# Retention and maxout FFN on one core: transposes moved, weight sums gathered in the first tile, the last product by token blocks

## The chip, the cores and the metric

One core of a Trainium2 chip. The metric is the device time of one execution in microseconds (us). Executions of one kernel spread over 0.5 to 4.3 us and the kernel before drifted from 832.8 to 835.7 us (medians) between sessions (four of the twelve experiments ran on a second chip, and are marked so), so small differences are read from the record's ratios and from positions inside the profiles.

Engine names in the profile: PE is TensorE (products), PEld its weight loads, DVE VectorE, ACT ScalarE, POOL GpSimd, SPq the queue of SyncE that issues the transfers here. "L435" is line 435 of that kernel's source; inserted lines shift the numbers between kernels, so the text gives the tile names too (x, dx, down, osb).

## The reference, cut to what matters

```python
# q, k, v: (8, 8, 576, 64) float32; w1, w2, w3: (512, 768); w_out: (768, 512), float64
scores = scale * np.matmul(q, k.transpose(0, 1, 3, 2))
ret = scores * Dmat                       # causal, decaying with distance
attn = np.matmul(ret, v)                  # -> x: 4608 tokens x 512
h = np.maximum(np.maximum(x @ w1, x @ w2), x @ w3)
return h @ w_out                          # 4608 x 512
```

## The kernel before

Attention runs in 36 chunks of 128 tokens, the FFN in 9 tiles of 512 tokens. The float64 weights arrive as bit patterns and are converted to float32 by VectorE, ScalarE and GpSimd while the first tile is computed in the plain way; the other eight tiles use sums and differences of weight blocks (seven products instead of eight). In the traces each engine runs its instructions in the order in which the program lists them: in the kernel before, ScalarE's copies of the fourth chunk start at 23.30 us, behind the conversion's passes at 21.92 and 22.68. The parts that matter here (cuts marked):

```python
BY_PE = 8     # chunks 0..7: q and k transposed by TensorE; later chunks by VectorE

def load(g):
    rows = (("k", k), ("q", q), ("v", v)) if g < BY_PE else (("k", k), ("v", v))
    for n, src in () if g < BY_PE else (("q", q), ("kx", k)):
        # [cut] 16 transfers of 16 KB each, in the layout that VectorE's transpose needs
    for n, src in rows:
        # [cut] one or two transfers of whole rows; v comes last

def decay_values(g):          # GpSimd: vd = v * decay; needs v of the chunk

def downs(t, h):              # second half of the FFN for a tile: seven products
    def product(n, out, first):
        for fp in range(NF // 2):
            for m in range(NM):           # NM = 2 token blocks of 128
                nc.tensor.matmul(out[:, m, :], lhsT=..., rhs=..., start=first and m == 0 and fp == 0, ...)
    x = ps_x.tile([P, NM, DM // 2], FP32, tag="x", name="dx")   # both blocks: one PSUM tile
    # [cut]
    product(3, x, False)
    total(0, 1, x, [])        # ScalarE copies x to osb, one transfer of 256 KB to the output

# first tile, down products m = 0..3: weight sums of units [0], [1], [2], [3, 4];
# second tile: the sums of units 5..8, one per unit

warm(6); load(0); load(1)
nc.sync.dma_start(gs[:], state_decay); nc.sync.dma_start(gq[:], out_decay)
# [cut]
scores(2); convert(2); transposes(3); values(2); convert(2); scores(3)
```

## Time and profile before

| what | value | where it is read |
|---|---|---|
| median time | 832.78 us (3 runs), 833.6 us (6 runs) | timed runs |
| span of the profiled execution | 834.0 us | page, first line |
| TensorE busy | 823.8 us, 99% | page, part 1 |
| holes in TensorE | 2.0, 1.4, 1.4, 1.2, 0.7 us | list of waits |
| last product ends, span ends | 830.45, 834.0 us | chain of waits |

How to read it: TensorE is the bound, so another engine's time counts only where TensorE waits for it. The list of waits gives "who waited for whom: us in total, times, longest". In a timeline a line is "start, duration, engine, line, operation, out<-in, count", and square brackets hold the idle time of that engine just before and what ended it. The lines themselves are shown in the prediction.

### The profile page before, as it was taken

How to read it: one execution, taken by the hardware profiler on the slowest of the kernel's cores; microseconds unless marked ns; L12 is line 12 of the kernel's file. 1: busy time of each engine (PE TensorE's matmuls, PEld its weight loads, DVE VectorE, ACT ScalarE, POOL GpSimd, SP SyncE). 2: the span in 40 equal slices, each digit the busy share in tenths (PEclk: the TensorE clock that was granted, in tenths of full speed). 3: DMA queues.
4: the chain of work that ended last, by engine and by line, in shares of the span. 5: the costliest groups of instructions: out<-in, count | busy, mean ns of one | idle time of the engine just before them, and what ended most of it. 6: DMA issues, size and time to landing. Idle time of an engine off the chain costs nothing.

```text
span 834.0 us, 12632 instructions
## 1 busy us (share of the span) xinstructions
PE 823.8 (99%) x4626; PEld 670.5 (80%) x4626; DVE 427.3 (51%) x803; ACT 174.7 (21%) x395; POOL 186.7 (22%) x182
## 2 busy tenths in 40 slices
PE   8899999999999999999999999999999999999998
PEld 8545556788888888888888888888888888888887
DVE  3879946754355443554444445544545435533341
ACT  2656721111111101111111111111111011111211
POOL 3535545511211130212011111111111202201000
PEclk9999999999999999999999999999999999999999
DMA  8946521334133323332233313332333223201001
GB/s 220 283 131 188 133 58 40 57 56 84 50 55 56 56 59 65 67 56 55 60 55 73 67 48 56 57 57 80 56 57 54 59 60 73 48 13 38 1 1 50
DMA packets 232509, 59.06 MB, mean 71 GB/s; under 512 B 213504, under 2 KB 230912, under 8 KB 232448
## 3 DMA queue, kind: packets, MB, share of 16 engines
q1 hardware_dynamic: 232304, 58.26, 31.1%
q8 instruction: 36, 0.59, 0.3%
q14 instruction: 25, 0.20, 0.1%
q10 hardware_dynamic: 144, 0.00, 0.0%
HBM read 48.76 MB, written 9.44 MB: 70 GB/s over the span
## 4 chain that ended last, share of the span: by engine, by line
PE 95%; DMA 2%; DVE 1%; SPq 1%; ACT 0%; POOL 0%; issue 0%; DVEq 0%
PE x L435 30%; PE z L435 15%; PE dx L311 10%; PE y L435 7%; PE up L493 7%; PE dz L311 5%; PE s L183 4%; PE o L213 4%; PE o L218 4%; PE kv L194 4%; PE dy L311 2%; PE down L484 2%; SPq L152 1%; DMA bits<-in_moe_w_dram 1%; DMA gs<-in_state_decay_dram 1%; SPq L146 1%
## 5 line engine op out<-in xcount | busy, mean ns | idle before, releaser
L435 PE MATMUL x<-S,T 128*128 128x256 f32 x576 | 147.9, 379 | 0.0
L435 PEld LDWEIGHTS x<-S,T 128*128 128x128 f32 x576 | 109.1, 190 | 15.4 <-ACT p L440 0.3
L156 POOL TENSOR_TENSOR vd<-vraw,gk 128x512 f32<-128x512 f32 x36 | 37.8, 1049 | 344.9 <-DMA vraw<-in_v_dram 319.4
L435 PE MATMUL x<-S,w 128*128 128x256 f32 x288 | 74.5, 381 | 1.2 <-DVE h L465 1.2
L435 PE MATMUL x<-xT,w 128*128 128x256 f32 x288 | 74.8, 382 | 0.0
L435 PE MATMUL z<-S,w 128*128 128x256 f32 x288 | 73.9, 379 | 0.0
L435 PE MATMUL z<-xT,T 128*128 128x256 f32 x288 | 73.9, 379 | 0.0
L435 PE MATMUL y<-xT,w 128*128 128x256 f32 x288 | 73.9, 379 | 0.0
L465 DVE TENSOR_TENSOR tmp<-x,p 128x256 f32<-128x256 f32 x48 | 20.4, 425 | 103.4 <-PE x L435 103.4
L440 ACT COPY p<-x 128x256 f32<-128x256 f32 x72 | 26.8, 372 | 221.0 <-PE x L435 221.0
L186 DVE TENSOR_TENSOR st<-s,causal 128x512 f32<-128x512 f32 x72 | 46.3, 685 | 44.6 <-PE s L183 44.6
L493 PE MATMUL up<-xT,w 128*128 128x512 f32 x144 | 63.8, 595 | 1.4 <-POOL w L387 1.4
L435 PEld LDWEIGHTS x<-S,w 128*128 128x128 f32 x288 | 49.3, 189 | 14.8 <-DVE h L465 1.8
L435 PEld LDWEIGHTS z<-S,w 128*128 128x128 f32 x288 | 54.7, 190 | 7.4
L435 PEld LDWEIGHTS y<-xT,w 128*128 128x128 f32 x288 | 54.7, 190 | 7.4
L435 PEld LDWEIGHTS z<-xT,T 128*128 128x128 f32 x288 | 54.3, 189 | 7.9
L220 DVE TENSOR_TENSOR xT<-o,gq 128x512 f32<-128x512 f32 x36 | 24.8, 690 | 67.9 <-PE o L218 62.4
L435 PEld LDWEIGHTS x<-xT,w 128*128 128x128 f32 x288 | 51.5, 190 | 6.6 <-issue 0.8
L493 PEld LDWEIGHTS up<-xT,w 128*128 128x128 f32 x144 | 26.6, 190 | 32.2 <-issue 29.9
L294 POOL TENSOR_TENSOR H<-h 128x256 f32<-128x256 f32 x24 | 18.1, 756 | 150.7 <-DVE h L478 150.0
L440 ACT COPY u<-x 128x256 f32<-128x256 f32 x72 | 26.8, 372 | 99.8 <-PE x L435 97.1
L183 PEld LDWEIGHTS s<-qT,kT 64*128 64x128 f32 x576 | 35.0, 187 | 15.6 <-issue 11.7
(92 smaller groups left out, 1210.1 us busy)
## 6 DMA issues: line engine op xcount, KB each, us to landing
bits<-in_moe_w_dram SPq DMA_DIRECT2D x18, 512.0 KB, 4.7
out_dram<-osb SPq DMA_DIRECT2D x36, 256.0 KB, 2.1
kraw<-in_k_dram SPq DMA_DIRECT2D x32, 256.0 KB, 3.0
vraw<-in_v_dram SPq DMA_DIRECT2D x32, 256.0 KB, 3.5
qraw<-in_q_dram SPq DMA_DIRECT2D x448, 16.0 KB, 1.8
kxraw<-in_k_dram SPq DMA_DIRECT2D x448, 16.0 KB, 1.8
bits<-in_moe_w_out_dram SPq DMA_DIRECT2D x6, 512.0 KB, 3.4
qraw<-in_q_dram SPq DMA_DIRECT2D x7, 256.0 KB, 4.4
```

Source lines behind the costliest of these rows:

```text
L156: nc.gpsimd.tensor_tensor(t[:], raws.pop(("v", g))[:], gk[:].unsqueeze(2).to_broadcast([C, H, D]), op=ALU.mult)
L183: nc.tensor.matmul(s[j][:, p, :], lhsT=kT[r, p, :], rhs=qT[r, p, :], start=True, stop=True)
L186: nc.vector.tensor_tensor(st[:, j], s[j][:], masks[start_of(g)][:].unsqueeze(1).to_broadcast([C, NP, C]), op=ALU.mult)
L194: nc.tensor.matmul(kv[:, p, :], lhsT=pair(kr, p)[r:], rhs=pair(vds[g], p)[r:], start=True, stop=True)
L213: nc.tensor.matmul(o[D * j:D * (j + 1), p, :], lhsT=vr[:, 2 * p + j, :], rhs=st[:, j, p, :], start=(p == 0), stop=(old == 0 and p == NP - ...
L218: nc.tensor.matmul(o[:, p, :old], lhsT=sd[:, p, :], rhs=qT[:, p, :old], start=False, stop=(p == NP - 1), skip_group_check=True)
L220: nc.vector.tensor_tensor(xT[t][:, :, i * C:(i + 1) * C], o[:], gq[:], op=ALU.mult)
L311: nc.tensor.matmul(out[:, m, :], lhsT=hS[n](fp)[:, m * P:(m + 1) * P], rhs=late["T"][n][:, fp, :], start=first and m == 0 and fp == 0, sto ...
L435: nc.tensor.matmul(out[:], lhsT=w[:, d * P:(d + 1) * P], rhs=xS[t][n][:, d, :], start=first and d == 0, stop=d == 1, skip_group_check=True)
L440: nc.scalar.copy(c[:], src[:])
L465: nc.vector.tensor_tensor(c22, x[:], p7[:], op=ALU.add)
L493: nc.tensor.matmul(ps[:], lhsT=w_sb[i, fb][:, dc * P:(dc + 1) * P], rhs=xT[t][:, dc, :], start=(dc == 0), stop=(dc == NDC - 1))
```

## The change

Its intent: close the holes at the front, take one more chunk's transposes off TensorE, get the weight sums out of the second tile's way, and let the first half of the last output leave while the second half is computed. The diff, cut to its core:

```diff
-BY_PE = 8
+BY_PE = 7
-    def load(g):
+    def load(g, *between):
         for n, src in rows:
+            if n == "v":
+                for t, what in between:
+                    nc.sync.dma_start(t[:], what)
# downs(), last product
-        product(3, x, False)
-        total(0, 1, x, [])
+        osb = opool.tile([P, NM, DM // 2], FP32, tag="osb", name="osb")
+        for m in range(NM):
+            product(3, x, False, [m])
+            nc.scalar.copy(osb[:, m, :], x[:, m, :])
+            nc.sync.dma_start(place(0, 1)[:, m, :], osb[:, m, :])
# ffn()
-                if t == 1:
-                    weight_sums(n + 5)
-                for n in [[0], [1], [2], [3, 4]][m]:
+                for n in [[0, 1, 2], [3, 4, 5], [6], [7, 8]][m]:
# start
-    load(1)
-    nc.sync.dma_start(gs[:], state_decay)
-    nc.sync.dma_start(gq[:], out_decay)
+    load(1, (gs, state_decay), (gq, out_decay))
-    warm(3)
+    warm(2)
-    convert(2)
     transposes(3)
+    convert(2)
# [cut: the helper place(), the argument blocks of product()]
```

More of the change, by code (lines that the diff above doesn't have):

```diff
@@ L302, in summed, with product @@
             return lambda fp: late["S"][n][:, fp, :]
+        NM = NH // P
         hS = {1: raw_hidden(0, 0), 2: raw_hidden(0, 1), 3: summed(4), 4: raw_hidden(1, 1),
               5: summed(1), 6: summed(2), 7: summed(3)}
-        NM = NH // P
-        def product(n, out, first):
+        def product(n, out, first, blocks=range(NM)):
             for fp in range(NF // 2):
-                for m in range(NM):
+                for m in blocks:
                     nc.tensor.matmul(out[:, m, :], lhsT=hS[n](fp)[:, m * P:(m + 1) * P], rhs=late["T"][n][:, fp, :],
@@ L320, in kept, with place @@
             return both
+        def place(r, c):
+            block = out[t * NT + r * NH:t * NT + (r + 1) * NH, c * (DM // 2):(c + 1) * (DM // 2)]
+            return block.rearrange("(m p) d -> p m d", p=P)
         def total(r, c, src, others):
@@ L325, in total @@
                 nc.vector.tensor_tensor(osb[:, m, :], src[:, m, :], o[:], op=ALU.add)
-            if not others:
-                nc.scalar.copy(osb[:], src[:])
-            block = out[t * NT + r * NH:t * NT + (r + 1) * NH, c * (DM // 2):(c + 1) * (DM // 2)]
-            nc.sync.dma_start(block.rearrange("(m p) d -> p m d", p=P), osb[:])
+            nc.sync.dma_start(place(r, c), osb[:])
         x = ps_x.tile([P, NM, DM // 2], FP32, tag="x", name="dx")
@@ L558 @@
     scores(2)
+    transposes(3)
     convert(2)
-    transposes(3)
     values(2)
```

## The prediction

> **What bounds the kernel now.** I read the page's first two parts first (busy shares and the 40 slices), then the list of waits of TensorE, then the chain of waits piece by piece, then the timelines of the other engines around each hole in TensorE.
>
> ```profile
> span 834.0 us, 12632 instructions
> PE 823.8 (99%) x4626; PEld 670.5 (80%) x4626; DVE 427.3 (51%) x803; ACT 174.7 (21%) x395; POOL 186.7 (22%) x182
> PEclk9999999999999999999999999999999999999999
> ```
>
> TensorE is busy for 823.8 of 834.0 us at an unthrottled clock. So a change can only (a) take work off TensorE, (b) close a hole in it, or (c) shorten the start or the end. The holes are few; the waits of TensorE, all of them:
>
> ```profile
> PE s L183 <- ACT qT L175: 2.0, 1, 2.0
> PE warm L113 <- POOL ident masks.py:199: 1.4, 1, 1.4
> PE up L493 <- POOL w L387: 1.4, 1, 1.4
> PE x L435 <- DVE h L465: 1.2, 1, 1.2
> PE s L183 <- DVE state L197: 0.7, 1, 0.7
> ```
>
> Four holes of 2.0, 1.4, 1.2 and 0.7 us are within the change's reach (the warm-up's 1.4 is not touched). After 35.03 us the timeline of TensorE has one hole only, the 1.2 us before 162.03, until the last product ends at 830.45. The rest, to 834.0, is the tail. The 2.0 us hole in the chain of waits:
>
> ```profile
> 14.57 5.89 DMA bits<-in_moe_w_dram
> 20.49 1.41 DVE expo L365
> 21.92 0.73 ACT expo L368
> 22.68 0.72 ACT expo L371
> 23.40 0.47 ACT kT L175
> 23.87 0.49 ACT qT L175
> 24.41 1.21 PE s L183 x16
> ```
>
> The fourth chunk's scores wait for copies that stand on ScalarE behind the first weight conversion, which itself waits for the weight bits to land at 20.46. Everything from there to the second up-product (35.03) hangs on that landing and then on VectorE, which in its timeline is idle from 24.32 to 25.60 and at no other time between 22.43 and 33.8:
>
> ```profile
> 23.64 0.68 DVE L381 SCALAR_TENSOR_TENSOR expo<-bits,expo 128x512 int32<-128x512 int32 x1
> 25.60 1.29 DVE L186 TENSOR_TENSOR st<-s,causal 128x512 f32<-128x512 f32 x2 [1.28 <-PE s L183]
> ```
>
> The 1.2 us hole, on VectorE's timeline:
>
> ```profile
> 156.05 1.44 DVE L478 TENSOR_TENSOR h<-h,tmp 128x512 f32<-128x512 f32 x1
> 157.41 0.94 DVE L414 TENSOR_TENSOR T<-w,w 128x256 f32<-128x256 f32 x1
> 158.39 0.83 DVE L415 TENSOR_TENSOR T<-w,T 128x256 f32<-128x256 f32 x1
> 159.15 0.70 DVE L167 STREAM_TRANSPOSE kT<-kxraw 128x512 f32<-128x512 f32 x1
> 159.77 0.66 DVE L167 STREAM_TRANSPOSE qT<-qraw 128x512 f32<-128x512 f32 x1
> ...
> 161.57 0.41 DVE L465 TENSOR_TENSOR h<-x,p 128x256 f32<-128x256 f32 x1
> ```
>
> VectorE has no gap here. The chain of waits names a q transfer landing at 159.14, but that one belongs to a later chunk and VectorE was at L415 until then, so I read the hole as a backlog: weight sums (L414, L415), transposes and hidden sums ahead of L465, which frees x. The tail:
>
> ```profile
> 830.48 0.58 ACT osb L327
> ...
> out_dram<-osb SPq DMA_DIRECT2D x4, 256.0 KB, 2.1
> ```
>
> **What the Trainium skill says.** "SBUF — State Buffer", section "Who interferes with whom": a VectorE instruction in a two-port mode, or with two SBUF inputs, and a GpSimd instruction that reads SBUF exclude each other, and the later one waits. The trace agrees: the same L365 takes 0.42 us alone and 1.40 us at 20.49, where GpSimd runs its state product from 20.32 to 21.60; L415 takes 0.42 alone and 1.37 beside GpSimd's sums. So weight sums moved close together will cost more than 0.42 each. "DMA: Bandwidth & Descriptors", section "Anatomy of one DMA": about 2.0 us fixed per transfer. The trace is near it: 16 KB pieces land in a median 1.8 us, the 256 KB output in 2.1, so halving the last output saves little of its landing. "TensorE: Matmul & The Clock Gate", Part 1: the array starts at half rate until it has been busy for some 3.4 us. Here four transposes take 1.06 us at 4.16 and 0.60 us at 9.26, so the dropped warm-up is a half-rate one.
>
> **The change part by part.**
>
> 1. Transposes of the fourth chunk ahead of the conversion. Only ScalarE's order changes: kT and qT are copied at about 20-21 us instead of 23.3-24.4. The 2.0 us hole closes, but the gain is not 2.0: scores then need VectorE for st, and VectorE must first finish L381. L381 needs the second exponent pass (ScalarE, ends 23.40), so it can start at 23.46 and not 23.64, and st at about 24.1 and not 25.60. VectorE is gap-free from there to the second piece's weights, so the second up-product comes 1.28 + 0.18 = about 1.45 us sooner (33.6). The 1.4 us hole behind it stays, since both its sides move.
>
> 2. gs and gq ahead of the second v, and one warm-up product fewer (1.30 us for three, so 0.43). The bytes ahead of v are then those ahead of gq before: v should land near 11.7 (gq's landing, 7.12 + 4.6) instead of 9.0, its decay product on GpSimd ends at 12.8, and the second kv may start at 12.85 instead of 13.08. So the 0.7 hole moves rather than goes, 0.2 us net. Even that is swallowed: the weight bits are the fifteenth transfer of the same queue in both orders, behind the same bytes, and part 1's chain starts at their landing. Gain to the end: 0.
>
> 3. Eighth chunk's transposes to VectorE. TensorE loses eight 128x128 transposes, from 108.15 to 109.02 in its timeline: 0.87 us, all on the path. ScalarE loses two copies. VectorE gains 0.70 + 0.66 = 1.36 us, in the new order behind its last conversion (109.6-110.2 before), near 109-110.3; the scores that need them start near 111.8. Slack about 1.5 us.
>
> 4. Weight sums of the last four units into the first tile. TensorE does nothing in them. VectorE moves 4 x 2 x 0.42 = 3.4 us and GpSimd 4 x about 1.65 = 6.6 us from the second tile into 108-134, where they were busy 16.3 and 16.05 of 26 us. In the second tile the pair L414, L415 at 157.41 goes, 1.74 us ahead of L465, which then ends near 160.25 on the old clock; TensorE wants it at 160.69. The 1.2 us hole closes: 1.18 us, with 0.4 us to spare.
>
> 5. Last product by token blocks. All twelve instructions (2.59 us) stay. The first block is copied and sent during the second's products. The last copy is 128x256: 0.37 us (L440) for 0.58, and the last transfer 128 KB, which I put at 1.9 us against 2.1. Gain 0.21 + 0.2 = 0.4 us, once.
>
> Sum: 1.45 + 0 + 0.87 + 1.18 + 0.4 = 3.9 us. From the median of 832.78: 828.9, and I say 829.0.
>
> **The rivals.**
>
> Rival A, the transfer queue takes it back. Chunk eight now loads as 32 pieces of 16 KB, each 0.47 us to issue: 15 us instead of some 3. Behind it in the same queue stand the last weight piece and chunk nine. Starting 1.45 us sooner (85.1): pieces until 100.2, k and v until 101.2, the last weight piece issued at 101.3 and landed near 105.7 (it was at 95.2). Its first VectorE use was at 106.12, so would be at 104.6: about 1.1 us late. Most of it drowns, as VectorE waits 0.7 and 0.9 us for TensorE around there; the last converted weights come at about 110.3 and the first down-product wants them at 111.0. Chunk nine's v then lands near 122 instead of 111, and on GpSimd the decay product of that v stands ahead of three weight-sum pairs and the S3 and S4 sums: 122 + 1.0 + 1.4 + 5.2 + 1.8 = 131.4 for S3, +1.4 for S4. The second tile's first use of S3 is near 134.1, of S4 near 136.7. Margin 2.7 us. If issue runs slower than 0.47 us (0.53 in one stretch, with waits), it shrinks to about 1. If it fails, a new hole of 1-2 us stands near 111 or 134, and the time is 830-831. I give that 0.2.
>
> Rival B, the front gains nothing, because the weight bits land later or a VectorE-GpSimd collision falls worse (each is worth 1.0 us, see L365). Then the time is about 830.4. Or a collision falls away, and it is 828.
>
> Rival C, the front gains the whole 2.0 + 0.7 + 0.43: only if the bits land earlier as well. The transfer engines moved under 160 GB/s in several half microseconds between 11.5 and 18.5, so it isn't excluded; the time would be about 827.5. Against it: the order of everything from the third chunk on is unchanged.
>
> Rival D, the hole at 162 is a landing after all, as the chain says; then moving the sums leaves it, and the time is 830.2.
>
> **Range and chances.** The profiled execution took 835.73 us against the median of 832.78, and one of three runs 836.51, so the front (the only part with transfers on the path) varies by 3 us, and part of the holes I count may be smaller in a typical run. I set 829.0, with 827.4 to 831.2 for 8 in 10. Two per cent is 16.7 us; no rival comes near it: within 2% 0.98, faster 0.01, slower 0.01.
>
> **What would show it.** Step 1: the scores of the fourth chunk start near 22.2 with no wait on the copies, VectorE's st near 24.1, the second up-product at 33.3-33.9. Step 2: a wait of the second kv for vd of about 0.9 us. Step 3: no transposes on TensorE near 107, no wait before the scores near 112, and the first down-product without a hole. Step 4: no wait of x on L465 near 160. Step 5: the last copy 0.37 us, the end 0.4 us sooner after the last product. TensorE's busy time should fall by about 1.3 us (0.87 and 0.43). I am wrong if the second up-product doesn't move, or if TensorE waits for w_out, S or kT between 105 and 140.

## The result, and the profile after

The changed kernel took 844.1 us (median of 6 runs, 843.43 to 845.47) against 833.6 us (6 runs, 832.24 to 836.51). The ratio is 1.0121, 95% interval 1.0099 to 1.0143: slower by 1.2%, inside the 2% band but far outside the predicted 827.4 to 831.2. (Ratios are the record's, this kernel over the kernel before, from fast runs, so not quite the ratio of the medians quoted. The second group of experiments, blocks with both copies afterwards, rows first, late transposes and late gs, has only one new run of the kernel before; the other seven are those of the first group.)

The page of the changed kernel, its first line and its first part's:

```profile
span 841.7 us, 12670 instructions
PE 827.1 (98%) x4616; PEld 669.1 (79%) x4616; DVE 427.3 (51%) x805; ACT 175.2 (21%) x401; POOL 184.8 (22%) x182
```

Ten instructions fewer on TensorE, yet it is busy for longer: one stretch ran at half the clock (below), and a group broken by a wait counts more busy time than a whole one (the two halves of dx have 1.46 and 1.56 us, the twelve of the kernel before 2.75). Its waits, all of them:

```profile
PE dx L313 <- ACT osb L358: 5.4, 8, 2.1
PE down L490 <- POOL w_out L393: 3.1, 3, 1.4
PE warm L113 <- POOL ident masks.py:199: 1.4, 1, 1.4
PE o L216 <- DVE st L189: 1.0, 2, 0.8
PE s L186 <- ACT qT L178: 0.2, 1, 0.2
```

Every hole that the change aimed at is gone (the one on qT is another, at the first chunk; the 1.0 us of o on st is what is left in place of the 2.0 us hole, as the fourth chunk's values now wait for VectorE). Two new ones stand on top: the last product (dx) waits for ScalarE's copy in each of eight tiles, and the first tile's down-product waits for converted output weights. To see what each costs I laid the two timelines of TensorE side by side and noted the start of the same instruction in both:

| instruction on TensorE | before, us | after, us | after less before |
|---|---|---|---|
| second up-product | 35.03 | 31.60 | -3.43 |
| first down-product | 109.02 | 104.72 | -4.30 |
| scores of the eighth chunk | 114.27 | 114.28 | +0.01 |
| first up-product after the tenth chunk's scores | 165.18 | 163.74 | -1.44 |
| dy product of the second tile | 203.51 | 202.42 | -1.09 |
| dy product of the eighth tile | 738.76 | 742.21 | +3.45 |
| dy product of the ninth tile | 814.74 | 822.28 | +7.54 |
| end of the span | 834.0 | 841.7 | +7.7 |

So the front gained 3.43 us (1.45 predicted), the transposes 0.87 (as predicted), the first down-product lost 4.31, and the hole at 162 gave 1.45 (1.18 predicted), of which 0.35 was lost again by the end of the second tile. From there the kernel lost 0.69 to 0.93 us in each of six tiles, 4.09 us in one, and 0.16 at the end: 8.8 us in all.

**The last product.** TensorE at the end of the second tile in the kernel before, then TensorE and ScalarE there in the changed kernel:

```profile
220.76 2.75 PE L311 MATMUL dx<-w_out,H 128*128 128x256 f32 x12
```
```profile
219.67 1.46 PE L313 MATMUL dx<-w_out,H 128*128 128x256 f32 x6
221.59 1.56 PE L313 MATMUL dx<-w_out,H 128*128 128x256 f32 x6 [0.46 <-ACT osb L358]
```
```profile
221.16 0.37 ACT L358 COPY osb<-dx 128x256 f32<-128x256 f32 x1 [7.94 <-PE dx L313]
```

The copy of the first block runs from 221.16 to 221.53, and only then, at 221.59, do the second block's products start. Six instructions at 0.216 us are 1.30 us, but 1.92 us lie between the two starts. The profile names ScalarE's copy as what released them, and the generated instructions agree: the second block's first product carries a semaphore wait on that copy, though the blocks share no element. They share a PSUM tile, and with it a bank. The Trainium skill has this in "PSUM — Partial Sum Buffer", section "PSUM bank collisions raise a hardware error": accesses of two engines to one bank must be guarded by bank and not by address. I had not looked it up. The trace agrees with the guard: 0.46 us of listed wait in seven of the eight tiles, 0.7 us of lost time in each. Whether the shared tile or the shared bank makes the tool that builds the program put the wait there is not shown: the experiment below that removes it changes both. (A build, not run, with one tile laid over two banks, still has the wait, which speaks for the tile.)

In the eighth tile it was worse. The chain of waits there, then the windows view (columns: stretch, length, busy time and count of PE, PEld, DVE, ACT and POOL, granted clock, DMA share, GB/s):

```profile
757.37 4.27 DMA out_dram<-osb
```
```profile
762.00:764.00 2.00, 1.83 (x7) 1.56 (x8) 0.00 (x0) 0.11 (x1) 0.00 (x0) 0.81 0.19 66
764.00:766.00 2.00, 2.00 (x6) 1.57 (x5) 0.00 (x0) 0.48 (x2) 0.00 (x0) 0.50 0.19 66
766.00:768.00 2.00, 2.00 (x9) 1.74 (x8) 0.42 (x1) 0.26 (x1) 0.00 (x0) 0.84 0.00 0
```

One output transfer took 4.27 us to land where the median is 2.1. The copy needed that transfer's buffer, and now TensorE waited behind the copy: 2.14 us instead of 0.46. After this hole the granted clock was at half: 2 x (0.19 + 0.50 + 0.16) = 1.7 us lost. Together 0.7 + 1.7 + 1.7 = 4.1, the tile's 4.09. The kernel before has such a landing too (4.1 us at most), and ScalarE's copy at 669.12 us waited for it, but TensorE did not wait behind that copy.

**The first down-product.** TensorE in the kernel before, then TensorE, GpSimd and the transfer queue in the changed kernel:

```profile
109.02 5.32 PE L484 MATMUL down<-w_out,h 128*128 128x512 f32 x12
```
```profile
106.93 2.35 PE L490 MATMUL down<-w_out,h 128*128 128x512 f32 x4 [0.33 <-POOL w_out L393]
110.72 1.12 PE L490 MATMUL down<-w_out,h 128*128 128x512 f32 x2 [1.44 <-POOL w_out L393]
113.22 1.13 PE L490 MATMUL down<-w_out,h 128*128 128x512 f32 x2 [1.37 <-POOL w_out L393]
```
```profile
91.81 1.28 POOL L393 TENSOR_TENSOR w_out<-mant,expo 128x512 f32<-128x512 f32 x1 [1.30 <-DVE expo L387]
103.39 1.04 POOL L159 TENSOR_TENSOR vd<-vraw,gk 128x512 f32<-128x512 f32 x1 [10.29 <-DMA vraw<-in_v_dram]
...
105.61 2.49 POOL L393 TENSOR_TENSOR w_out<-mant,expo 128x512 f32<-128x512 f32 x2
```
```profile
91.14 7.54 SPq L146 DMA_DIRECT2D kxraw<-in_k_dram  x16
...
99.25 0.53 SPq L155 DMA_DIRECT2D vraw<-in_v_dram  x1
99.88 0.86 SPq L260 DMA_DIRECT2D bits<-in_moe_w_out_dram  x1
```

Of the 4.31 us lost here 3.1 are listed as waits. GpSimd idles for 10.29 us before the eighth chunk's decay product, because that chunk's v was issued behind 32 small pieces and landed at 103.3. The last four conversions of output weights stand behind it on GpSimd, and VectorE in turn waits for them (4.13 us idle before 106.91, for the buffers that they free).

### The profile page after: what moved, and what is told of

The parts are those of the page before. It is cut to its first block, busy times and chain, and to the rows that moved or that the text cites. A ratio compares the mean times of both kernels' runs of the same rounds, so it can differ in the third digit from the quotient of the medians.

```text
span 841.7 us, 12670 instructions
## 1 busy us (share of the span) xinstructions
PE 827.1 (98%) x4616; PEld 669.1 (79%) x4616; DVE 427.3 (51%) x805; ACT 175.2 (21%) x401; POOL 184.8 (22%) x182
## 4 chain that ended last, share of the span: by engine, by line
PE 92%; SPq 2%; DMA 2%; DVE 2%; issue 1%; ACT 0%; POOL 0%; POOLq 0%; DVEq 0%; ACTq 0%
PE x L441 30%; PE z L441 15%; PE dx L313 10%; PE y L441 7%; PE up L499 5%; PE dz L313 5%; PE s L186 4%; PE o L216 4%; PE o L221 4%; PE kv L197 4%; PE dy L313 2%; SPq L146 2%; PE down L490 2%; DMA bits<-in_moe_w_dram 1%; DMA bits<-in_moe_w_out_dram 1%
## 5 line engine op out<-in xcount | busy, mean ns | idle before, releaser
L460 DVE TENSOR_TENSOR tmp<-y,p 128x256 f32<-128x256 f32 x48 | 20.4, 425 | 52.9 <-PE y L441 52.9
```

What stands on the lines that cost most here:

```text
L460: nc.vector.tensor_tensor(c11, y[:], p1[:], op=ALU.add)
```

## The experiments

Two theories from the traces, each to be tried against its rival. Theory 1: the last product by blocks costs about 8.8 us through the wait on the copy. Theory 2: the eighth chunk's v, late in the queue, costs 4.3 us. Every kernel was correct.

### The last product whole again

```diff
-        for m in range(NM):
-            product(3, x, False, [m])
-            nc.scalar.copy(osb[:, m, :], x[:, m, :])
-            nc.sync.dma_start(place(0, 1)[:, m, :], osb[:, m, :])
+        product(3, x, False)
+        nc.scalar.copy(osb[:], x[:])
+        nc.sync.dma_start(place(0, 1), osb[:])
```

> The changed kernel with its last product done whole again (both token blocks, one copy, one transfer, as before). Theory 1: the second block's products wait for ScalarE's copy of the first (0.73 us in each of eight tiles, 3.4 us more in the last but one where the copy waited for a transfer and the clock fell to half), less 0.57 us at the tail: 7.7 + 1.1 = some 8.7 us comes back, about 835.2 us, and no wait of dx on the copy remains, nor the half-rate stretch near 763. Rival: the second half of the program is slowed by the granted clock whatever the product order: then it stays above 840.

Measured: 835.63 us, ratio to before 1.0009 (0.9985 to 1.0033), against 1.0121 for the changed kernel. No wait of dx is left, and no half-rate stretch in the later tiles; the rival falls. In this profile there was a half-rate stretch at the first down-product instead (two instructions took 2.07 us, 1.13 in the changed kernel's profile, after the same two holes of 1.44 and 1.37 us), so a hole's price varies from run to run.

### The eighth chunk back on TensorE

```diff
-BY_PE = 7
+BY_PE = 8
```

> The changed kernel with the eighth chunk on TensorE again. Theory 2: the first down-product loses 4.3 us because the eighth chunk's v lands behind 32 small pieces (its decay product on GpSimd idles 10.3 us and four weight conversions stand behind it); undone, 4.3 us comes back and 0.87 us of transposes is paid: 844.1 - 3.4 = about 840.7. Rival: those holes come from weight sums or VectorE's transposes: then 844 to 845.

Measured: 840.11 us, ratio 1.0069 (1.0051 to 1.0087). The waits of down on w_out are gone, the eight waits of dx stay (5.1 us listed). As expected by theory 2; gathered weight sums alone make no hole.

### Both undone

The two edits above together.

> Both undone: only the front and the weight sums of the change are left. If the two theories add up: 833.6 - 3.4 (front) - 1.1 (hole at 162) = about 829.0. Rival: they overlap (a hole closed opens another), 831 or more.

Measured: 830.95 us, ratio 0.9960 (0.9940 to 0.9981): 3.3 us faster than before, not the 4.5 that I had added up from one profile each and close to the rival's 831, but faster. Its list of waits has a new one, the second kv on vd, of 0.6 us. What is left of the change is a gain.

### The kernel before, with the last product by blocks alone

```diff
-        product(3, x, False)
-        total(0, 1, x, [])
+        for m in range(NM):
+            product(3, x, False, [m])
+            nc.scalar.copy(osb[:, m, :], x[:, m, :])
+            nc.sync.dma_start(block[:, m, :], osb[:, m, :])
```

> The kernel before with the last product by blocks alone. Theory 1: 0.73 x 8 - 0.57 - 0.73 hidden nowhere = 5.3 us slower (838.9), or 8.7 us (842.3) if the long landing in the last but one tile and the half-rate stretch come with it. Rival (the loss needs the rest of the change): 833.6.

Measured: 842.32 us, ratio 1.0102 (1.0077 to 1.0127). This one part makes the loss by itself, without anything else of the change. In its profile the hole behind a slow landing stood in the seventh tile (2.40 us) and the clock stayed full; in two others, the changed kernel and the one with the eighth chunk back on TensorE, the pair comes with the half rate:

```profile
673.26 1.56 PE L311 MATMUL dx<-w_out,H 128*128 128x256 f32 x6 [2.40 <-ACT osb L356]
```

### Blocks in order, both copies afterwards

```diff
         for m in range(NM):
             product(3, x, False, [m])
+        for m in range(NM):
             nc.scalar.copy(osb[:, m, :], x[:, m, :])
             nc.sync.dma_start(place(0, 1)[:, m, :], osb[:, m, :])
```

> The changed kernel with the last product still in block order, but both copies (and both transfers) after the second block. Theory 1, narrowed: the loss is the wait of the second block on the copy of the first, not the block order: no wait of dx, time as with the whole product, 835 to 836 less up to 0.4 us at the tail. Rival: the order of the products itself costs (weight loads, switching between blocks): the time stays near 842-844.

Measured: 835.93 us, ratio 1.0021 (0.9992 to 1.0050), with no wait of dx. The order of the products costs nothing that can be seen; the copy between them does.

### Rows of k and v ahead of the small pieces

```diff
-        for n, src in () if g < BY_PE else (("q", q), ("kx", k)):   # small pieces first
-        for n, src in rows:
+        for n, src in rows:                                         # whole rows first
+        for n, src in () if g < BY_PE else (("q", q), ("kx", k)):
```
(on the kernel with the whole last product, eighth chunk on VectorE)

> The changed kernel with the whole last product, and for chunks transposed by VectorE the k and v rows issued ahead of the 32 small pieces. Theory 2, narrowed: v of the eighth chunk landing late is the cause of the holes at the first down-product; early, GpSimd no longer idles 10 us, the holes go, 4.3 us comes back from 835.6: 831.3, or 0.9 us below the kernel with both undone (830.1). Rival: the last weight piece, which is as late as before, holds the down-product too: 834 or more, with a wait of down on w_out left.

Measured: 831.93 us, ratio 0.9972 (0.9956 to 0.9988). Theory 2 holds for the larger part: GpSimd no longer idles before the eighth chunk's decay product, which starts at 94.88. But the rival is right as well, in small: one wait of down on w_out is left, 1.1 us, and VectorE shows its cause:

```profile
106.86 0.43 DVE L370 TENSOR_SCALAR expo<-bits 128x512 int32<-128x512 int32 x1 [2.27 <-DMA bits<-in_moe_w_out_dram]
```

The last weight piece is still issued behind the 32 small ones, at 103.02. This is the prediction's rival A, with the effect that it gave it ("a new hole of 1-2 us stands near 111"), though this order issues the piece 3.1 us later than the changed kernel does (99.88 there).

### Small pieces behind the last weight piece

```diff
-                        load(g + 1)
+                        load(g + 1, pieces=g + 1 != BY_PE)      # eighth chunk: k and v rows only
+                    if step is scores and g + 1 == BY_PE:
+                        load(g + 1, whole=False)                # its small pieces, one step later
```

> Whole last product, eighth chunk on VectorE, its k and v rows ahead of the last weight piece and its 32 small pieces behind it. Theory 2: both late transfers are then in time, no wait of down on w_out or of scores on kT is left near 105-115, and the 0.87 us of transposes is at last a gain: 831.0 (both undone) - 0.9 = about 830.1. Rival: the pieces now land too late for VectorE's transposes (needed near 109-111), a wait of scores takes the gain back: 831 or more.

Measured: 830.79 us, ratio 0.9943 (0.9927 to 0.9959). No wait of down and none of scores near 105 to 115 is left; the twelve instructions of the first down-product run from 106.14 without a break. So two transfers have to be early here, v and the last weight piece. (Second chip, as the next experiment and the last two of this part.)

### The last tile's blocks in two banks

```diff
+        if t == N // NT - 1:
+            x = apart = [ps_x.tile([P, DM // 2], FP32, tag="x", name="dx")[:],
+                         ps_r.tile([P, DM // 2], FP32, tag="r", name="dx1")[:]]
+        # last tile: product by blocks, a copy and a transfer after each; other tiles: whole
```
(on the kernel of the experiment before)

> The same, and in the last tile only the last product by blocks, with the two blocks' sums in two PSUM tiles of their own banks. Theory 1: the wait on the copy is put there because both blocks lie in one PSUM tile; apart, the second block doesn't wait and the tail alone is shorter by 0.4 to 0.6 us: about 829.6. Rival: a wait of 0.46 us stays (the engine's, not the tile's): no gain or a loss of 0.2.

Measured: 829.73 us, ratio 0.9932 (0.9917 to 0.9947), in the same rounds as the one before (0.9943), and the fastest kernel. Its chain of waits and ScalarE's timeline at the end:

```profile
823.45 2.60 PE dx L313 x12
```
```profile
824.79 0.37 ACT L368 COPY osb<-dx 128x256 f32<-128x256 f32 x1 [5.83 <-PE dx L313]
826.08 0.37 ACT L368 COPY osb<-dx 128x256 f32<-128x256 f32 x1 [0.92 <-PE dx L313]
```

The first copy lies inside the twelve instructions, which run through: with a tile and a bank each there is no wait. From the last product's end to the span's end it is 829.0 - 826.05 = 2.95 us, where the whole product of the experiment before has 829.8 - 826.17 = 3.63: 0.7 us at the tail. The intervals of the two ratios overlap, so the gain in time is indicated and the missing wait is shown. The clock has a part in the ratio to the kernel before: of that kernel's eleven runs here, eight had a mean granted clock of 0.997 or 0.998 and took 835.56 to 837.37 us, three had 1.000 and took 833.10 to 834.05, while all six of this kernel had 1.000. Against the three alone the gain is 3.7 us.

### Transposes behind the conversion again

```diff
-    transposes(3)
     convert(2)
+    transposes(3)
     values(2)
```
(on the kernel with both undone)

> The kernel with both undone (830.95 us), and the fourth chunk's transposes back behind the first conversion. If the transposes carry the front's gain: 1.5 to 3 us slower than that kernel (832.5 to 834), the 2.0 us wait of the scores on the copies is back. Rival (the gs order carries it): within 0.5 us of 831.

Measured: 832.95 us, ratio 0.9989 (0.9968 to 1.0010), 0.0029 or 2.4 us above the kernel with both undone, but from other rounds. The wait is back, and in this profile (836.16 us, the slowest of six) the granted clock was 0.50 from 26 to 28 us, behind it:

```profile
PE s L186 <- ACT qT L178: 2.8, 1, 2.8
```

In its own rounds the next kernel, which has the transposes early, stands at 0.9965, 2.0 us better, with overlapping intervals. So that this part carries most of the front's gain is indicated by the time, and the wait is shown.

### gs and gq behind the second v again

> The kernel with both undone, and gs and gq back behind the second v. The prediction's step 2 says 0: 830.5 to 831.5, with the 0.7 us wait on the state back. Rival: the weight bits land some 0.5 us later and a GpSimd collision of 1.3 us comes back: 831.5 to 833.

(On the kernel with both undone: the two transfers issued after the second chunk's three.) Measured: 831.53 us, ratio 0.9965 (0.9948 to 0.9982), against 0.9960 with the order changed. The wait of scores on the state is back (1.1 us), and the end does not move by more than the intervals. The prediction's "gain to the end: 0" is not contradicted; half a microsecond either way can't be told.

### Three warm-up products again

> The kernel with both undone, with the third warm-up product back. The prediction's step 2 says 0: 830.5 to 831.5. Rival: the weight bits are issued and land earlier with the earlier start (they landed at 20.01 in the changed kernel against 20.46 before): then 0.4 us slower, 831.4.

(On the kernel with both undone.) Measured: 831.22 us, ratio 0.9946 (0.9930 to 0.9962); nominally faster than with two, in other rounds. No gain of the dropped warm-up is to be seen.

### Weight sums of the last units back in the second tile

```diff
-                for n in [[0, 1, 2], [3, 4, 5], [6], [7, 8]][m]:
+                for n in [[0], [1], [2], [3, 4]][m]:
+                if t == 1:
+                    weight_sums(n + 5)
```
(on the kernel with both undone)

> The kernel with both undone, and the weight sums of the last four units back in the second tile. The prediction's step 4: the 1.2 us hole on L465 near 160 comes back: 1.1 us slower, about 832.1. Rival (the hole was a landing of a transfer): no hole either way, 831.0.

Measured: 831.79 us, ratio 0.9958 (0.9942 to 0.9973); in the same rounds the three-warm-up kernel, which differs in this part, had 0.9946, so 1.0 us apart with overlapping intervals. The hole is back, at its place:

```profile
158.19 1.13 PE L440 MATMUL x<-S,w 128*128 128x256 f32 x4 [1.02 <-DVE h L470]
```

No other kernel with gathered sums has it. It was VectorE's backlog and not a landing: rival D falls.

## Why the prediction was wrong, point by point

- **Step 5, the last product by blocks: the step that failed.** It said "The first block is copied and sent during the second's products." The opposite happened: the second block waited for the copy, 0.7 us in each of eight tiles, and once per run a slow landing was added to it, in some runs with a stretch at half clock. I priced the part as a gain of 0.4 us "once", at the tail, and did not ask what it does in the eight tiles where it also stands; the instruction list of the changed kernel shows the wait on ScalarE. It cost 8.8 us in the profile and 1.0% alone on the kernel before. Its tail term was right: the span ends 0.57 us sooner after the last product, 0.4 was said (last copy 0.37 us, transfer 1.7 us in the median where I put 1.9).
- **Rival A: the right queue, the wrong transfer.** I followed the last weight piece and the ninth chunk's v behind the 32 small pieces, and gave them 0.2. The eighth chunk's own v stands there too, and GpSimd takes its decay product ahead of four weight conversions. That cost 4.3 us at the first down-product. The hole came where I said it would ("near 111"), and so did the sign of being wrong that I had named, a wait for w_out between 105 and 140, but by a mechanism beside the one I computed. With v early, the last weight piece makes a hole of 1.1 us by itself. No wait on S or kT came.
- **Step 1, the transposes first: right, but too small.** Scores start at 21.13 (22.2 was said) without a wait on the copies, VectorE's st at 23.47 where I said 24.1. The second up-product came 3.43 us sooner, not 1.45. VectorE and GpSimd at that point:

```profile
23.47 1.28 DVE L189 TENSOR_TENSOR st<-s,causal 128x512 f32<-128x512 f32 x2
```
```profile
29.90 1.65 POOL L393 TENSOR_TENSOR w<-mant,expo 128x512 f32<-128x512 f32 x1 [1.90 <-DVE expo L387]
```

  st moved by 2.13 us: 0.45 of it because the weight bits landed at 20.01 and not at 20.46, which step 2 had called fixed, the rest mostly from the closed gap. This is not steady either: in the profiles VectorE's first use of the bits lies between 19.96 and 21.34, with two warm-up products as with three. Another 1.28 us came because the second piece's GpSimd product took 1.65 us, not 2.94. That is a collision that fell away, the lucky half of rival B. It is not a steady gain: the list of waits has the 1.4 us hole on w again in four of the eleven profiles that have the early transposes.
- **Step 2: its end not contradicted, its sign missed.** Undoing either piece moved the end by less than the intervals. But the 0.9 us wait of the second kv for vd isn't in the changed kernel's list: the decay product starts at 10.79, so v landed about 0.9 us sooner than the 11.7 that I had put.
- **Step 3: its own term right.** 0.87 us left TensorE's path (-3.43 to -4.30 in the table). Once v and the last weight piece were in time, VectorE's slack was enough and the gain stays in the positions: from the second up-product to the first down-product it is 73.1 us in that kernel (33.03 to 106.14), 74.0 before. In the time it is not seen: 0.9943, against 0.9946 in the same rounds for the kernel with three warm-up products and these transposes on TensorE.
- **Step 4: right.** The hole closed, 1.45 us for 1.18, and came back when the sums went back (1.0 us).
- **The sum.** Predicted -3.9. Measured from profile to profile: -3.43 - 0.87 + 4.31 - 1.45 + 0.35 + 8.63 + 0.16 = +7.7. The gains came out larger than predicted, 5.75 us; the two new waits took 13.1.

What stays open: why in each profiled execution an output transfer takes up to 4.1 to 5.5 us to land (the runs show only that it happens in the kernel before too), and whether it was the tile or the bank that brought the wait.

## What to carry to other kernels

Before splitting a product so that its first half can leave early, look at where the halves lie: here two halves in one PSUM tile, and so in one bank, were serialised against the engine that read them, at 0.7 us a time, and two in tiles and banks of their own were not. Split only where the tail is (the last tile) and not in every tile. When a load turns from one large transfer into many small ones, list everything issued behind them in the same queue and, on each engine, everything that stands behind the instruction that waits for them. The version that does both, with the rest of the change, is 0.7% faster than the kernel before (0.9932); the clock has a part in this ratio, as said there.

## What the Trainium skill lacked or had wrong

- "TensorE: Matmul & The Clock Gate", section "Why this matters for your kernels", asks for no idle gaps above some 3 us between products. Here the granted clock fell to 0.50 after a hole of 2.14 us (changed kernel, eighth tile) and after two holes of 1.44 and 1.37 us close together (last product whole again), while a hole of 2.40 us in another kernel left it at 1.00. So a shorter gap can be enough, and not every one is.
- "DMA: Bandwidth & Descriptors", section "Anatomy of one DMA — SWDGE (gpsimd) path", gives a fixed cost of some 2.0 us, measured on transfers that GpSimd issues, and no spread of landings. Here, with SyncE issuing, outputs land in a median of 2.1 us at 256 KB and 1.7 us at 128 KB, and every profile has one whose landing took 4.1 to 5.5 us.
- "PSUM — Partial Sum Buffer", section "PSUM bank collisions raise a hardware error", has a rule that fits and gives no price for obeying it. Here it was 0.46 us of wait and 0.7 us of lost time for a copy of 0.37 us between two halves of one tile.
